# First layer of a spatial-shift mixer regrouped into three tiles of 128 channels and one of 64, with the gate logits moved to VectorE

## The chip, the cores and the metric

The kernel runs on one NeuronCore of a Trainium2 chip. The metric is device microseconds of the whole program, the median of several runs. Engine names are those of the profile: PE is TensorE, PEld its weight load, DVE is VectorE, ACT is ScalarE, POOL is GpSimd, SP is SyncE, which here does nothing but issue DMAs in order.

## What is computed

For one sequence of 2048 tokens with 448 channels, the reference mixes two branches by a gate per token:

```python
g = sigmoid((x * gate_w).sum(-1, keepdims=True))
a = A_ref(x, ...)              # S4D: long convolution over the tokens, per channel
h = gelu(layernorm(x) @ w1)    # 448 -> 448
# h in 4 groups of 112 channels, shifted by +1, -1, +2, -2 tokens
x1 = x + shifted(h) @ w2
b = x1 + gelu(layernorm(x1) @ w3) @ w4     # 448 -> 1792 -> 448
return g * a + (1 - g) * b
```

## The kernel before, in words

The tokens are taken in four blocks of 512 (`TB`). The work is a list of 72 **units**. Units 0 to 15 are the mixer, four per block, one per shift group, in the order of groups 0, 2, 1, 3. Units 16 to 71 are the MLP, 14 slices of 128 hidden channels per block. Each unit has a first layer (`first`, L437) and a second layer (`second`, L499). Precision is kept by splitting every operand into a high and a low part (`xh`+`xl`, `w1h`+`w1l`, `uh`+`ul`). A first layer is therefore 11 matmuls of 512 columns: four K tiles of `xh` with the high weights, four with the low weights, and three of `xl` with the high weights. A second layer is 12 matmuls of 448 columns: `uh` with high weights, `uh` with low weights, `ul` with high weights, for each of the four 128-token tiles `j`.

Between a unit's two layers lies a **hand-over** on two other engines. For a mixer unit DVE multiplies the PSUM result by the row of reciprocal standard deviations `rb` (`act_mul`, L446), ACT applies gelu (L456), ACT copies to the high part `uh` (L468), and DVE subtracts to get the low part `ul` (`act_tail`, L472). The main loop runs two units ahead (`LAG = 2`): its iteration n issues `first(n + 2)`, the hand-over of unit n + 2 up to `uh`, and `second(n)`. For n below 15 `act_tail(n + 1)` comes after the list `after` of iteration n, and from 15 on first of all. Every engine works its own queue strictly in the order of the program, so all that is put ahead of an `act_tail` on DVE delays the `ul` that PE waits for. At the end of a block, DVE adds the four accumulators to `xs` (L505, L508), and the next block's first `second` writes those PSUM banks again.

What comes at which iteration is written by hand, with calls `at(n, fn, ...)` in lists `before`, `after`, `between` and `late`. Four such jobs matter here. `stats_b` are LayerNorm statistics on DVE (L286, L288). `norm_turn` and `norm_fetch` transpose a tile of 128 tokens on DVE into a buffer of the two-deep pool tag `u`, write it to DRAM in two DMAs (`xd`) and read it back (`xr`). `ssm_par`, `ssm_exp`, `ssm_scale_par` and `ssm_moment` prepare the S4D branch: ACT takes an exponential of a 1 MB parameter load `pk`, DVE computes `dts` by a chain of small instructions, ACT scales by it (L580), and DVE reduces moments. `OWN = 34` is the first iteration of the S4D scans. Iterations before the fourth are written out in `begin()`.

The gate logits were an extra output column of the first layer: `w1` carried `gate_w` twice behind the 112 columns of a group, ACT copied the PSUM rows 96 to 113 of the units with group 0, and of the last with group 1 (`logits`, L540), and one row went through DRAM to `lt`. `gates()` turned it by a PE transpose, applied a sigmoid at iteration 15, and made `gs = 1 - g`. `weigh` (ACT, L410) multiplies `xs` by `gs`.

Of the kernel before, what the change touches and what calls it, by code (L numbers as in the profile page):

```python
# [24 lines left out]
GW = G + 2  # L25
# [4 lines left out]
SHIFT = (1, -1, 2, -2)  # L30
EPS = 1e-5
LAG = 2
OWN = 34
# [12 lines left out]
def gated_mix_kernel(tc, x, xT, xb, x0, w1, w2, w3, w4, par, logdt, dskip, ident, parg, uflip, lags, out):  # L46
    nc = tc.nc
    with tc.tile_pool(name="keep", bufs=1) as keep:
# [3 lines left out]
        with ExitStack() as ctx:  # L52
            mixer_and_small_steps(ctx, tc, xs, gg, okm, x, xT, xb, x0, w1, w2, w3, w4, par, logdt, dskip, ident, out)
# [121 lines left out]
def mixer_and_small_steps(ctx, tc, xs, gg, okm, x, xT, xb, x0, w1, w2, w3, w4, par, logdt, dskip, ident, out):  # L175
# [7 lines left out]
    def f32(ap):  # L183
        return ap.bitcast(F32)
# [7 lines left out]
    lg = dr.tile([1, L + 2], F32, name="lg")  # L192
# [16 lines left out]
    nu = big.tile([128, 4, 4], F32, name="nu")  # L209

# [30 lines left out]

    w1h, w1l = wpair([128, 4, 4, GW], "w1")
    w2h, w2l = wpair([G, 4, D], "w2")
    w1r = big.tile([128, 4, 4, GW], F32, name="w1r", tag="w4al")
    w2r = big.tile([128, 4, D], F32, name="w2r", tag="w4ah")

    def first_loads():
# [5 lines left out]
        act(w1r[:, 0], w1[:, 0])  # L253
        sp(r[:, :2 * HW], x0[:, :2 * HW])
        act(w1r[:, 2], w1[:, 2])
# [3 lines left out]
        sp(w1r[:, 1], w1[:, 1])  # L259
# [3 lines left out]
        sp(w1r[:, 3], w1[:, 3])  # L263
# [6 lines left out]
    def constants():  # L270
# [7 lines left out]
        nc.gpsimd.memset(carry, 0.0)  # L278
        nc.gpsimd.memset(rb[:, 0:HALO], 0.0)
# [139 lines left out]
    def first(n, bank="p1", seq=None, stop=True):  # L419
# [3 lines left out]
        if kind == "a":  # L423
            m = GW if i < 2 else G
            wh, wl = w1h[:, i, :, :m], w1l[:, i, :, :m]
            o = HALO - SHIFT[i]
        else:
            m = 128
            wh, wl = (w[:, :, i * m:(i + 1) * m] for w in (w3h, w3l))
            o = 0  # L430
# [4 lines left out]
        every = [(w, x_, k, 0, TB) for w, x_, r in ((0, 0, 4), (1, 0, 4), (0, 1, 3)) for k in range(r)]  # L435
        for q, (w, x_, k, t0, t1) in enumerate(seq or every):
            nc.tensor.matmul(p[:m, t0:t1], (wl if w else wh)[:, k, :], (xl if x_ else xh)[:, k, o + t0:o + t1],  # L437
                             start=(q == 0 and fresh), stop=stop if q + 1 == len(seq or every) else False)

    def act_mul(n):  # L440

        kind, b, i = units[n]
        m = G if kind == "a" else 128
        UF[n] = wk.tile([128, TB], F32, name="uf")
        o = b * TB + HALO - SHIFT[i]
        nc.vector.tensor_mul(UF[n][:m], P1[n][:m], rb[:m, o:o + TB])  # L446

    def act_head(n, later=False):
        kind, b, i = units[n]
        m = G if kind == "a" else 128  # L450
        UL[n] = wk.tile([128, TB], F32R, name="ul", bufs=3)
        UH[n] = wk.tile([128, TB], F32R, name="uh", bufs=3)
        if kind == "a":
            if n not in UF:
                act_mul(n)
            nc.scalar.activation(UF[n][:m], UF[n][:m], AF.Gelu_apprx_tanh)  # L456
        else:
            UF[n] = wk.tile([128, TB], F32, name="uf")
            nc.scalar.activation(UF[n][:m], P1[n][:m], AF.Gelu_apprx_tanh)  # L459
        if not later:  # L460
            act_copy(n)
        p = P1.pop(n)
        if kind == "a" and n and (i == 0 or (i == 1 and b == NB - 1)):
            logits(p, b, i)

    def act_copy(n):
        m = G if units[n][0] == "a" else 128
        nc.scalar.activation(UH[n][:m], UF[n][:m], AF.Copy)  # L468

    def act_tail(n):  # L470
        m = G if units[n][0] == "a" else 128
        nc.vector.tensor_sub(UL[n][:m], UF.pop(n)[:m], f32(UH[n][:m]))  # L472
# [9 lines left out]
    def second(n):  # L482
        kind, b, i = units[n]
        if kind == "a":
            wh, wl, m = w2h[:, i, :], w2l[:, i, :], G
            s, e = i == 0, i == 3
        else:
            wh, wl = W4[i]
            m = 128
            s, e = i == 0, i == NF - 1  # L490
        for j in range(NT):
            if s:
# [4 lines left out]
        for j, p in q:  # L497
# [550 lines left out]
```

## Time and profile before

| | us |
|---|---|
| Median of 3 runs | 380.78 (380.06 to 381.04) |
| Profiled execution | 380.4 |
| Its span in the trace | 378.6 |
| PE busy | 368.5 |
| DVE busy | 295.8 |
| ACT busy | 210.2 |

The span counts from the first to the last recorded instruction of the profiled execution; 1.8 us of its device time lie around it. Busy shares are averages over stages with different limits, so the prediction below reads single stretches. A row of the timeline gives start and duration in us, the engine and line, the operation, output and inputs with their shapes, a count, and in brackets the idle time before it with what ended it.

### The profile page before, as it was taken

The numbers are of one execution on the slowest core, as the hardware profiler recorded it, in microseconds if no ns is written. First come the engines' busy times: TensorE is split into PE (matmuls) and PEld (weight loads), VectorE is DVE, ScalarE is ACT, GpSimd is POOL, SyncE is SP. The second block draws the span as 40 slices with busy tenths as digits, with TensorE's granted clock in tenths as the row PEclk, the third lists the DMA queues.
The fourth block names the chain that finished last, engine by engine and source line by source line (L and its number), as shares of the span: only waits on it lengthen the run. The fifth ranks groups of instructions, "written<-read, shape, count | busy, mean of one in ns | idle before, by whom it ended". The sixth has DMA issues, their size and how long they took to land.

```text
span 378.6 us, 5180 instructions
## 1 busy us (share of the span) xinstructions
PE 368.5 (97%) x1713; PEld 314.6 (83%) x1713; DVE 295.8 (78%) x527; ACT 210.2 (56%) x349; POOL 71.1 (19%) x187
## 2 busy tenths in 40 slices
PE   7998999999999999999999999999999999999993
PEld 4786888888888888888888888888888888888883
DVE  4888979785858981998399989999787999996312
ACT  4764646546978467643465575465756654442220
POOL 3200070322000000040023536324041440000000
PEclk9999999999999999999999999999999999999998
DMA  8970606166615219000843515256685311372202
GB/s 266 397 265 1 224 1 173 30 118 209 209 56 157 46 50 214 3 0 12 243 72 78 83 29 153 63 160 124 97 183 134 78 28 19 73 189 48 77 0 102
DMA packets 85896, 42.26 MB, mean 112 GB/s; under 512 B 67030, under 2 KB 80614, under 8 KB 85226
## 3 DMA queue, kind: packets, MB, share of 16 engines
q1 hardware_dynamic: 85434, 41.20, 41.6%
q10 hardware_dynamic: 432, 0.70, 0.6%
q8 instruction: 15, 0.25, 0.3%
q14 instruction: 15, 0.12, 0.1%
HBM read 30.86 MB, written 11.02 MB: 111 GB/s over the span
## 4 chain that ended last, share of the span: by engine, by line
PE 90%; DVE 3%; ACT 2%; DMA 2%; issue 1%; POOL 0%; SPq 0%; DVEq 0%
PE p L437 46%; PE acc L499 43%; DMA w1r<-w_in 2%; PE acc L520 1%; ACT uh L468 1%; ACT uf L456 1%; PE misc L336 0%; DVE uf L446 0%; DVE z L638 0%; DVE w2l L218 0%; DVE b L286 0%; ACT w2h L217 0%; ACT xn L294 0%; DVE ul L472 0%; DVE xh L365 0%
## 5 line engine op out<-in xcount | busy, mean ns | idle before, releaser
L459 ACT ACTIVATE uf<-p 128x512 f32<-128x512 f32 x56 | 33.4, 597 | 101.9 <-PE p L437 101.8
L472 DVE TENSOR_TENSOR ul<-uf,uh 128x512 fp32r<-128x512 f32 (+1 forms) x72 | 48.9, 680 | 31.5 <-ACT uh L468 31.4
L638 DVE TENSOR_TENSOR_SCAN z<-z,carry 128x512 f32<-128x512 f32 x48 | 61.5, 1281 | 4.6 <-ACT z L633 0.7
L437 PE MATMUL p<-xh,w3h 128*128 128x512 f32 x224 | 61.3, 396 | 0.0
L437 PE MATMUL p<-xh,w3l 128*128 128x512 f32 x224 | 60.7, 392 | 0.0
L499 PE MATMUL acc<-w4h,uh 128*128 128x448 f32 x216 | 55.8, 364 | 0.3 <-DVE xs L508 0.3
L499 PE MATMUL acc<-w4h,ul 128*128 128x448 f32 x216 | 55.7, 364 | 0.0
L499 PE MATMUL acc<-w4l,uh 128*128 128x448 f32 x216 | 55.7, 363 | 0.0
L437 PEld LDWEIGHTS p<-xh,w3l 128*128 128x128 f32 x224 | 42.1, 188 | 9.9
L437 PE MATMUL p<-xl,w3h 128*128 128x512 f32 x168 | 48.0, 394 | 0.0
L437 PEld LDWEIGHTS p<-xh,w3h 128*128 128x128 f32 x224 | 42.0, 188 | 6.7
L468 ACT ACTIVATE uh<-uf 128x512 fp32r<-128x512 f32 (+1 forms) x72 | 45.6, 633 | 2.3
L499 PEld LDWEIGHTS acc<-w4h,uh 128*128 128x128 f32 x216 | 40.5, 188 | 6.6 <-issue 0.7
L499 PEld LDWEIGHTS acc<-w4l,uh 128*128 128x128 f32 x216 | 40.5, 188 | 3.1
L499 PEld LDWEIGHTS acc<-w4h,ul 128*128 128x128 f32 x216 | 40.5, 188 | 2.9
L633 ACT ACTIVATE z<-zs,nu 128x512 f32<-128x512 f32 x64 | 42.2, 710 | 0.8 <-DMA zs<-xT_in 0.4
L632 POOL COPY z<-carry 128x1 f32<-128x1 f32 x48 | 34.6, 731 | 17.4 <-DVE zs L644 17.1
L437 PEld LDWEIGHTS p<-xl,w3h 128*128 128x128 f32 x168 | 31.5, 188 | 7.2
L323 POOL TENSOR_TENSOR t<-r 128x4 f32<-128x4 f32 (+1 forms) x15 | 6.8, 453 | 133.2 <-DVE r L321 132.5
L640 POOL COPY carry<-z 128x1 f32<-128x1 f32 x48 | 14.1, 294 | 92.4 <-DVE z L638 91.5
L456 ACT ACTIVATE uf<-uf 112x512 f32<-112x512 f32 x16 | 10.1, 630 | 24.2 <-DVE uf L446 24.1
L638 DVE TENSOR_TENSOR_SCAN z<-z,carry,zero 128x512 f32<-128x512 f32 x16 | 20.0, 1247 | 0.0
(150 smaller groups left out, 496.5 us busy)
## 6 DMA issues: line engine op xcount, KB each, us to landing
zs<-xT_in SPq DMA_DIRECT2D x4, 1024.0 KB, 8.1
yd<-yt SPq DMA_DIRECT2D x56, 64.0 KB, 2.0
ysb<-yd SPq DMA_DIRECT2D x16, 224.0 KB, 3.0
out_dram<-xs SPq DMA_DIRECT2D x16, 224.0 KB, 2.8
raw<-xb_in SPq DMA_DIRECT2D x3, 1032.0 KB, 7.9
raw<-w_in SPq DMA_DIRECT2D x3, 1024.0 KB, 5.6
xd<-xt SPq DMA_DIRECT2D x16, 192.0 KB, 2.1
xr<-xd SPq DMA_DIRECT2D x16, 192.0 KB, 3.5
```

The costliest lines, as they stand in the source:

```text
L323: eng.tensor_mul(t, y, y)
L437: nc.tensor.matmul(p[:m, t0:t1], (wl if w else wh)[:, k, :], (xl if x_ else xh)[:, k, o + t0:o + t1], start=(q == 0 and fresh), stop=stop ...
L456: nc.scalar.activation(UF[n][:m], UF[n][:m], AF.Gelu_apprx_tanh)
L459: nc.scalar.activation(UF[n][:m], P1[n][:m], AF.Gelu_apprx_tanh)
L468: nc.scalar.activation(UH[n][:m], UF[n][:m], AF.Copy)
L472: nc.vector.tensor_sub(UL[n][:m], UF.pop(n)[:m], f32(UH[n][:m]))
L499: nc.tensor.matmul(ACC[j], (UL if p == 2 else UH)[n][:m, t], wl if p == 1 else wh, start=s and p == 0, stop=e and p == 2)
L520: nc.tensor.matmul(ACC[j], (UL if p == 2 else UH)[m][:, t], wl if p == 1 else wh, start=False, stop=m > n and p == 2)
L632: nc.gpsimd.tensor_copy(z4[:, m, 0:1], carry[:, k, m:m + 1])
L633: nc.scalar.activation(z4[:, m, 1:], ZS[b][:, k, :], AF.Copy, scale=nu[:, k, m:m + 1])
L638: nc.vector.tensor_tensor_scan(z, z, up, carry[:, k, m:m + 1], OP.add, OP.add)
L640: nc.gpsimd.tensor_copy(carry[:, k, m:m + 1], z[:, TB - 1:])
```

## The change

**Channels.** The 112 channels of group 2 (shift +2) are no longer a tile of their own. 16 of them go to the first 16 columns of each of the three other tiles, which so have 128, and the remaining 64 form the fourth tile, still the second unit of each block (units 1, 5, 9, 13). Its high and low weights stand side by side as 128 columns of one operand `w1d`, and its `uh` and `ul` stand above each other as 128 rows of one operand, against second-layer weights that are repeated in rows 64 to 127. **Fold.** The two halves of its PSUM result must be added (`act_add`): ACT copies the lower half, DVE adds.

**Edge columns.** The 16 guest channels of the other tiles need another shift than their hosts. ACT writes the gelu of the whole tile, then for rows 0 to 15 overwrites the first 1 to 4 columns from a carried tile `skew` and the other 508 to 511 columns shifted, and copies the last 4 columns to `skew`. The very first tokens get their values from four small matmuls (`first_tokens`, `first_skew`). The gelu of these units goes to a tile `ug` with one buffer.

**Gates.** `x` is read again, a tile of 448 channels for 128 tokens at a time, into the `u` buffers, and DVE sums its product with `gate_w` (`gate_sum`). The logistic function is made from Exp on ACT, and an addition and a reciprocal on DVE.

**Places.** The statistics of block 1 move from iterations 10 and 12 to 15 and 16; the second half of the S4D preparation moves two iterations later, and so does `OWN`; `begin()` is reordered.

```diff
-        every = [(w, x_, k, 0, TB) for w, x_, r in ((0, 0, 4), (1, 0, 4), (0, 1, 3)) for k in range(r)]
+        every = [(w, x_, k, 0, TB) for w, x_, r in ((0, 0, 4), (1, 0, 4), (0, 1, 3)) for k in range(r)
+                 if not w or wl is not None]
...
+    def act_add(n):
+        p = P1[n]
+        UF[n] = wk.tile([128, TB], F32, name="uf")
+        nc.scalar.activation(UF[n][:GD], p[GD:], AF.Copy)
+        nc.vector.tensor_add(UF[n][:GD], p[:GD], UF[n][:GD])
...
     def act_head(n, later=False):
...
-            nc.scalar.activation(UF[n][:m], UF[n][:m], AF.Gelu_apprx_tanh)
+            o, sk = SHIFT[2] - SHIFT[i], skew[:, TI[i], :]
+            uf, UF[n] = UF[n], big.tile([128, TB], F32, name="ug", tag="w4bl")
+            nc.scalar.activation(UF[n], uf, AF.Gelu_apprx_tanh)
+            nc.scalar.activation(UF[n][:GX, :o], sk[:, SKEW - o:], AF.Gelu_apprx_tanh)
+            nc.scalar.activation(UF[n][:GX, o:], uf[:GX, :TB - o], AF.Gelu_apprx_tanh)
+            if b + 1 < NB:
+                nc.scalar.activation(sk, uf[:GX, TB - SKEW:], AF.Copy)
...
-        if kind == "a" and n and (i == 0 or (i == 1 and b == NB - 1)):
-            logits(p, b, i)
...
     def act_tail(n):
...
+        if kind == "a" and i == 2:
+            nc.vector.tensor_sub(UH[n][GD:], uf[:GD], f32(UH[n])[:GD])
...
-        q = [(j, p) for p in range(3) for j in range(NT)]
+        q = [(j, p) for p in range(2 if kind == "a" and i == 2 else 3) for j in range(NT)]
...
+    def gate_fetch(j):
+        GX_[j] = wk.tile([128, 512], F32, name="gx", tag="u")
+        nc.sync.dma_start(GX_[j][:, :D], x[j * 128:(j + 1) * 128])
+
+    def gate_sum(j):
+        t = GX_.pop(j)[:, :D]
+        nc.vector.scalar_tensor_tensor(t, t, 1.0, GR[0], op0=OP.mult, op1=OP.mult, accum_out=gg[:, j:j + 1])
...
     def gates():
-        p = ps.tile([128, L // 128], F32, name="misc", bufs=1)
-        nc.tensor.transpose(p, LT[0], idt[:L // 128, :L // 128])
-        nc.scalar.activation(gg, p, AF.Sigmoid)
+        nc.scalar.activation(gg, gg, AF.Exp, scale=-1.0)
+        nc.vector.tensor_scalar(gg, gg, 1.0, None, op0=OP.add)
+        nc.vector.reciprocal(gg, gg)
...
+        first(3, "misc", wh_wl[5:])
+        first_tokens()
...
+        keep_warm(2)
...
+        act_add(5)
         stats_b(2 * NT + 1, 2 * NT + 3)
         act_head(4)
...
-    for b, (n, m, q) in enumerate(((5, 6, 6), (10, 12, 12), (27, 28, 29), (34, 35, 36))):
+    for b, (n, m, q) in enumerate(((5, 6, 6), (15, 16, 17), (27, 28, 29), (34, 35, 36))):
...
+    for j, n in zip(range(L // 128), (16, 16, 17, 17, 19, 19, 20, 20, 23, 23, 24, 24, 25, 25, 26, 26)):
+        at(n, gate_fetch, j, when=late)
+        at(n + 1, gate_sum, j)
...
-    at(25, ssm_exp, 1)
+    at(27, ssm_exp, 1)
+    at(27, gates)
...
+                if units[n + LAG][::2] == ("a", 2):
+                    act_add(n + LAG)
```

How the instructions stand at three places follows, from the order of the program on each engine; a row is the line, the operation, the output and inputs, and the output's shape.

**First place: PE, the first layer of unit 5**, the second unit of block 1 (`p_423` before, `p_442` of the change). Before:

```order
L437 MATMUL p_423<-xh,w1h 112x512 x4
L437 MATMUL p_423<-xh,w1l 112x512 x4
L437 MATMUL p_423<-xl,w1h 112x512 x3
```

Of the change:

```order
L450 MATMUL p_442<-xh,w1d 128x512 x4
L450 MATMUL p_442<-xl,w1d 128x512 x3
```

The four matmuls with the low weights are gone, since those are columns of `w1d`.

**Second place: DVE at the end of `begin()`**, from the last row of the second rstd to the accumulators of block 0. Before:

```order
L310 SCALAR_TENSOR_TENSOR r_82<-t,r_82 128x4
L286 BN_STATS b_441<-xs 128x6 x2
L288 BN_AGGR st<-b_441 128x2 x2
L446 TENSOR_TENSOR uf<-p_392,rb 112x512
L446 TENSOR_TENSOR uf<-p_423,rb 112x512
L472 TENSOR_TENSOR ul<-uf,uh 112x512
L505 TENSOR_TENSOR xs<-acc_316,xs 128x448
```

Of the change:

```order
L324 SCALAR_TENSOR_TENSOR r_81<-t,r_81 128x4
L512 TENSOR_TENSOR ul<-ug,uh 128x512
L457 TENSOR_TENSOR uf<-p_442,uf 64x512
L300 BN_STATS b_459<-xs 128x6 x2
L302 BN_AGGR st<-b_459 128x2 x2
L473 TENSOR_TENSOR uf<-p_408,rb 128x512
L469 TENSOR_TENSOR uf<-uf,rb 64x512
L512 TENSOR_TENSOR ul<-ug,uh 128x512
L544 TENSOR_TENSOR xs<-acc_330,xs 128x448
```

The tail of unit 3 (`ul` in the second row) and the fold of unit 5 (`p_442`) now stand ahead of the multiplication of unit 4 (`p_408`).

**Third place: the DMA queue of SP at iterations 19 and 20.** `xd` are the transposed tiles on their way to DRAM, `xr` is their way back, `gx` the second read of `x`. Before:

```order
L390 DMA xd<-xt 128x3x128
L392 DMA xd<-xt 128x64
L390 DMA xd<-xt 128x3x128
L392 DMA xd<-xt 128x64
L397 DMA xr<-xd 128x12x32
L400 DMA xr<-xd 64x4x32 x2
```

Of the change:

```order
L404 DMA xd<-xt 128x3x128
L406 DMA xd<-xt 128x64
L404 DMA xd<-xt 128x3x128
L406 DMA xd<-xt 128x64
L584 DMA gx<-x_in 128x448 x2
L411 DMA xr<-xd 128x12x32
L414 DMA xr<-xd 64x4x32 x2
```

Two reads of `x` come between the two ways, into the buffers that the `xt` tiles leave.

More of the change, by code (lines that the diff above doesn't have):

```diff
@@ L480, in done, with second @@
             nc.sync.dma_start(out[q * 128:(q + 1) * 128], xs[:, q, :])
-    def second(n):
+    def second(n, part=slice(0, None)):
         kind, b, i = units[n]
         if kind == "a":
-            wh, wl, m = w2h[:, i, :], w2l[:, i, :], G
+            wh, wl = w2h[:, i, :], w2l[:, i, :]
             s, e = i == 0, i == 3
@@ L719, in keep_warm @@
         for _ in range(m):
-            nc.tensor.matmul(p[:GW], w1h[:, 0, 0, :], XH["a", 0][:, 0, :TB], start=True, stop=True)
+            nc.tensor.matmul(p, w1h[:, 0, 0, :], XH["a", 0][:, 0, :TB], start=True, stop=True)
     PS = []
```

242 lines of the change are left out of this document (142 added, 100 removed).

## The prediction

> **What bounds the kernel now.** I read the page's busy times and slices first, then its chain of work that ended last, then the groups of waits, then the timelines of PE and DVE between 35 and 152 us, where the change acts.
>
> ```profile
> PE 368.5 (97%) x1713; PEld 314.6 (83%) x1713; DVE 295.8 (78%) x527; ACT 210.2 (56%) x349; POOL 71.1 (19%) x187
> PE   7998999999999999999999999999999999999993
> PEclk9999999999999999999999999999999999999998
> PE 90%; DVE 3%; ACT 2%; DMA 2%; issue 1%; POOL 0%; SPq 0%; DVEq 0%
> ```
>
> PE is busy for 97% of the span, at full clock, and holds 90% of the chain. So a matmul taken away is worth its whole length, provided that what the others hand to PE is early enough to keep it fed. How early that is, three stretches of one mixer block each show (columns: stretch, its us, then busy us of PE, PEld, DVE, ACT, POOL):
>
> ```profile
> 38.13:58.43 20.30, 20.30 (x98) 17.14 (x96) 16.96 (x38) 11.86 (x21) 7.08 (x26) 1.00 0.33 112
> 58.43:78.61 20.18, 20.18 (x96) 17.03 (x95) 16.60 (x34) 10.81 (x18) 3.90 (x12) 1.00 0.38 100
> 78.61:98.80 20.19, 20.19 (x94) 17.08 (x93) 14.15 (x26) 13.19 (x19) 4.70 (x14) 1.00 0.63 171
> ```
>
> PE never stops there, but DVE works 14 to 17 of 20 us, and its remaining time is mostly waiting for ACT, since a unit passes DVE, ACT, ACT, DVE in turn. This second chain is close behind PE.
>
> **The change part by part: matmuls removed (A).**
>
> ```profile
> 43.23 2.55 PE p L437 x11
> 50.79 2.42 PE acc L499 x12
> ```
>
> A first layer takes 2.55 us for 11 matmuls, 0.232 each; a second layer 2.42 us for 12, 0.202 each. The four units with 64 channels lose four matmuls in each layer: 16 x 0.232 + 16 x 0.202 = 3.7 + 3.2 = **6.9 us**. Every other unit keeps its counts, as the duration of a matmul follows its columns and not its rows. The four small matmuls of the first tokens, two fewer of `keep_warm` and the lost PE transpose of the gates I take together at 0; between nothing and 0.3 us each way, as they stand where PE waits for data in the start.
>
> **The hand-over of units 4 to 15 (B).**
>
> ```profile
> L446 DVE TENSOR_TENSOR uf<-p,rb 112x512 f32<-112x512 f32 x16 | 10.9, 686 | 3.4 <-ACT rb L337 3.1
> L456 ACT ACTIVATE uf<-uf 112x512 f32<-112x512 f32 x16 | 10.1, 630 | 24.2 <-DVE uf L446 24.1
> L472 DVE TENSOR_TENSOR ul<-uf,uh 112x512 fp32r<-112x512 f32 x16 | 11.0, 685 | 3.4 <-ACT uh L468 3.3
> L540 ACT ACTIVATE lr<-p 18x512 f32<-18x512 f32 x5 | 3.0, 592 | 0.1
> L555 ACT ACTIVATE gg<-misc 128x16 f32<-128x16 f32 x1 | 0.2, 185 | 0.0
> L288 DVE BATCH_NORM_AGGREGATE st<-b 128x2 f32<-128x6 f32 x28 | 4.2, 174 | 0.1
> ```
>
> The row of 18x512 shows that a copy of 18 rows costs ACT 592 ns, near the 630 ns of a gelu of 112 rows: ACT is paid by columns. The shifted gelu of 16 rows by 508 to 511 columns is thus estimated at 0.66 us, like a full one, and the one of 1 to 4 columns at 0.10 to 0.19 us (the 128x16 row is 185 ns). Together **0.76 us** more between gelu and copy, in all units but the 64-channel ones; bounds 0.69 and 0.85.
>
> By the Trainium skill ("ScalarE: Activation LUTs", section "Rules for kernel authors") an ACTIVATE costs about 0.3 us and 0.83 ns per element. That would make the pair an estimated 1.02 us, and add about 1.6 us over the six waits; the 592 and 185 ns of the two rows speak for less.
>
> Next I followed the DVE order of the change from unit 4 to unit 15 with such durations, and compared each moment with before. The rows that carry it:
>
> ```profile
> 36.55 1.29 DVE L446 TENSOR_TENSOR uf<-p,rb 112x512 f32<-112x512 f32 x2
> 38.61 0.69 DVE L472 TENSOR_TENSOR ul<-uf,uh 112x512 fp32r<-112x512 f32 x1 [0.76 <-ACT uh L468]
> 54.32 0.69 DVE L446 TENSOR_TENSOR uf<-p,rb 112x512 f32<-112x512 f32 x1 [1.41 <-ACT rb L337]
> 80.38 1.15 DVE L286 BATCH_NORM_STATS2 b<-xs 128x6 f32<-128x448 f32 x2
> 95.62 1.29 DVE L472 TENSOR_TENSOR ul<-uf,uh 112x512 fp32r<-112x512 f32 x2
> 96.79 0.36 PE L499 MATMUL acc<-w2h,ul 112*128 112x448 f32 x1
> ```
>
> Terms, as later (+) or earlier (-) along DVE. At the start +0.2: the tail of unit 3 and the fold come ahead of the multiplication of unit 4 (+2.5), but the second rstd stands 2.3 us earlier. The row at 38.61 shows DVE waiting 0.76 us for ACT already, so ACT's added work comes straight out at the tails: 0.73, 0.5, 0.55, 0.14, 0.45, 0.14 and 0.9 us at units 4, 6, 7, 8, 10, 12 and 14 to 15, in all +3.4. The folds of units 9 and 13 are one DVE operation of 0.7 each, +1.4. Two subtractions of weights and `xl`, whose high parts ACT now copies later, +1.1. Against this, the wait of 1.41 us for `rb` at unit 8 is taken up (-1.4), and two calls of block 1's statistics leave (each 1.15 + 2 x 0.17 = 1.5, by the row at 80.38), -2.9. Sum 0.2 + 3.4 + 1.4 + 1.1 - 4.3 = **+1.8 us at the tail of unit 15**. In before this tail ends at 96.9 - 0.6 = 96.3, as the two that begin at 95.62 take 1.29 with their overlap, and PE takes that `ul` at 96.79: 0.5 us to spare. So unit 15's second layer ends **1.3 us later** than before, though PE has 6.9 us less to do: the hand-over eats all of A, in stalls that I put at 2.4 us ahead of the second layer of unit 4 and 1 to 1.5 us ahead of 8, 11, 12 and 15. Bounds: the saving comes through whole (-6.9), or 0.85 for the edges and nothing credited for `rb` (+3.5).
>
> **The S4D preparation (C).**
>
> ```profile
> 109.37 0.16 DVE L573 TENSOR_SCALAR dts<-dts 128x4 f32<-128x4 f32 x1
> 109.55 1.71 ACT L580 ACTIVATE pk<-pk,dts 128x256 f32<-128x256 f32 x4 [2.44 <-DVE dts L573]
> 111.28 1.28 ACT L459 ACT_TABLE_LOAD   x1
> 112.57 0.60 ACT L459 ACTIVATE uf<-p 128x512 f32<-128x512 f32 x1
> 113.21 0.63 ACT L468 ACTIVATE uh<-uf 128x512 fp32r<-128x512 f32 x1
> 113.87 0.69 DVE L472 TENSOR_TENSOR ul<-uf,uh 128x512 fp32r<-128x512 f32 x1 [4.34 <-ACT uh L468]
> 116.25 0.97 PE L499 MATMUL acc<-w4h,uh 128*128 128x448 f32 x4
> L668 DVE SCALAR_TENSOR_TENSOR xs<-ysb,gg,xs 128x448 f32<-128x448 f32 x16 | 10.1, 672 | 0.0
> L594 DVE DVE_READ_ACCUMULATOR mw<-mw 128x1 f32 x12 | 1.0, 82 | 0.0
> ```
>
> ACT stands still for `dts`, then scales, loads a table and only then forms `uf` and `uh` of unit 19: `uh` is there 113.84 - 109.53 = 4.3 us after `dts`, and PE takes it at 116.25, 2.4 us later. Ahead of `dts` on DVE now come the moved statistics (2.9 us with their rstd's share 0.4: 3.3) and two sums of gates, each like the 672 ns row and an 82 ns read, 1.5 with gaps; 1.1 of it fits into idle time, and DVE is 1.8 behind from B: 3.3 + 1.5 - 1.1 + 1.8 = 5.5, of which I take 5.2 as the statistics partly overlap. PE is 1.3 late and has 2.4 of slack: 5.2 - 1.3 - 2.4 = **+1.5 us**. Bounds 0 (DVE waits elsewhere give it back) and 2.5.
>
> **The gates (D).**
>
> ```profile
> xd<-xt SPq DMA_DIRECT2D x16, 192.0 KB, 2.1
> ysb<-yd SPq DMA_DIRECT2D x16, 224.0 KB, 3.0
> 120.01 0.39 SPq L390 DMA_DIRECT2D xd<-xt  x1
> 121.72 0.68 DVE L472 TENSOR_TENSOR ul<-uf,uh 128x512 fp32r<-128x512 f32 x1
> 139.33 0.65 DVE L472 TENSOR_TENSOR ul<-uf,uh 128x512 fp32r<-128x512 f32 x1
> 140.93 0.39 SPq L565 DMA_DIRECT2D pk<-par_in  x1
> 142.54 0.69 DVE L472 TENSOR_TENSOR ul<-uf,uh 128x512 fp32r<-128x512 f32 x1 [1.36 <-ACT uh L468]
> 146.37 0.63 ACT L568 ACTIVATE pk<-pk 128x512 f32<-128x512 f32 x1 [2.56 <-DMA pk<-par_in]
> 147.98 0.69 DVE L586 TENSOR_REDUCE rho<-pk 128x2 f32<-128x512 f32 x1 [4.74 <-ACT pk L580]
> ```
>
> The fetches of tiles 4 and 5 wait for the `u` buffers until the `xd` transfers have read them (120.01 + 2.1, in before's time), and land 3.0 us after (the row of the same 224 KB), near 125.1. DVE comes to their sums right behind the tail of unit 21, at 122.4 to 122.8: a new wait of some 2.3 us, with the tails of 22 and 23 and eight moment operations behind it, on which ACT in turn depends. SP's queue holds the `xr` issues behind these two fetches, so they move by up to 1.6 us as well. The fetches of tiles 8 and 9 stand behind the 1 MB `pk`, which took 146.37 - 140.93 = 5.4 us, while DVE reaches their sums near 140 to 141, after the tail at 139.33: a wait of 4 to 6 us. Part falls into idle time that is there (1.36 and 4.74 us in these rows), and the tails of 22 to 28 have some 5 to 9 us to spare, so that not all reaches PE. Last, the Exp of the gates on ACT waits for the sixteenth sum, with the gelu of unit 29 behind it, about 2 us. Traced to the end the delays give 0 to +6; I take **+3.5**, a little over the middle, because two of the three waits follow each other inside ten units and the slack can be spent only once. Sixteen sums (12 us of DVE) are otherwise hidden, and so is the S4D queue moved by two units: DVE idles at the end.
>
> **Sum:** 380.4 (profiled execution, 0.4 under the median) + 1.3 + 1.5 + 3.5 = 386.7; with up to 0.3 us back from the start, **386.5 us**.
>
> **The rivals.** *PE stays the bound*: DVE's idle time before the tails hides the edge work, PE runs through, and the gates fit into idle time. 380.4 - 6.9 + 0.5 = **374.0**, faster. It decides if the tail of unit 15 lands before PE reaches the third matmul of that unit, that is if B's +1.8 is in truth about -5. For it: DVE's busy time per block leaves 3 to 6 us. Against: most of those are waits for ACT, which gets longer. If half of A comes through and the rest is hidden, it is 377.
>
> *Only the mixer's hand-over counts*: A eaten, C and D lie in DVE's idle time (4.34, 1.36 and 4.74 us in the rows above), 380.4 + 1.3 = **381.7**, between 378.5 and 383.
>
> *The clock falls*. In before the slices show full clock and the longest wait of PE in the mixer is 1.1 us; here stalls of 2.4 us, up to 3.9, would stand. If the clock halved for one first layer after such a stall, 2.55 us would be added to the forecast: 386.5 + 2.5 = **389.0**.
>
> ```profile
> 35.23 0.65 PE L336 MATMUL misc<-idt,r 128*128 128x128 f32 x4 [1.15 <-DVE r L310]
> ```
>
> The Trainium skill ("TensorE: Matmul & The Clock Gate", section "What's actually happening") says that an idle window of about 3.4 us halves the clock. No stall of before is long enough to show it.
>
> **How the numbers follow.** My forecast, a hand-over that eats A plus stalls in units 17 to 29 (383 to 390.5), has 0.56; PE-bound 0.20 (half of it under 377); only the mixer 0.16; the clock 0.05; beyond 390.5, 0.03. The range of **377 to 390.5** leaves out 0.10 below and 0.03 above. A measurement tells 0.3%, or 1.1 us, from no change: 379.6 to 381.9 holds 0.09, about half of the second rival; faster is the first rival and a part of the second, 0.24; slower is the rest, 0.67.
>
> **What would show it.** A: PE's busy time falls by 7. B: PE idle ahead of the second layers of 4, 8, 11, 12 and 15, released by `ul` or the accumulators' addition; if unit 15 ends near 92 us, the first rival holds. C: ACT idle longer than 2.44 us for `dts`, and PE waiting ahead of unit 19. D: DVE idle with `gx` as releaser at tiles 4, 5, 8 and 9; if there is none, the second rival. A clock under 1.00 in any slice after 40 us shows the third. The forecast is wrong above all if the edge operations cost much less than a full gelu.

## The result, and the profile after

The changed kernel takes 396.07 us (395.88 to 397.36), the kernel before 380.91 in the same session: ratio 1.041, interval 1.038 to 1.044. It is **slower by 15.2 us**. Slower was forecast, but at 386.5 us and in a range that ended at 390.5.

The rows of the page that answer to the first ones of before:

```profile
PE 368.3 (93%) x1686; PEld 311.6 (79%) x1686; DVE 309.2 (78%) x568; ACT 215.2 (55%) x379; POOL 73.5 (19%) x193
PE   7989799889999998698999999999999999999994
PEclk9999899999999999899999999999999999999999
PE 62%; DVE 18%; ACT 9%; DMA 6%; issue 3%; SPq 0%; DVEq 0%; ACTq 0%
```

PE issues 27 instructions fewer, but is busy as long as before, since time at half its clock counts as busy too (without any such time it was busy 364.5 us in the first run below); it has holes in slices 5, 8, 9, 16, 17 and 19 (9.85 us each), and its clock fell in the fifth and the seventeenth. It holds 62% of the chain instead of 90%; DVE, ACT and DMA took the rest. Who stopped whom, from the groups of waits (total, times, longest):

```profile
ACT xn L396 <- DVE xh L388: 8.1, 4, 6.9
DVE gx L588 <- DMA gx<-x_in: 13.0, 5, 7.1
ACT pk L618 <- DVE dts L611: 5.9, 1, 5.9
PE p L450 <- DVE w3l L224: 3.9, 1, 3.9
PE acc L538 <- DVE xs L544: 2.4, 1, 2.4
PE acc L538 <- DVE ul L512: 2.4, 3, 1.2
```

PE waits for DVE, and DVE waits 13.0 us for tiles of `x` that it did not need before. The main stalls behind the start, in order of time, from PE's timeline (idle time ahead of the row and what ended it in brackets):

```profile
41.64 0.71 PE L538 MATMUL acc<-w2h,uh 128*128 128x448 f32 x1 [2.41 <-DVE xs L544]
77.24 0.47 PE L538 MATMUL acc<-w2h,ul 128*128 128x448 f32 x1 [1.24 <-DVE ul L512]
83.38 0.44 PE L538 MATMUL acc<-w2h,uh 128*128 128x448 f32 x1 [1.33 <-ACT uf L481]
100.18 0.47 PE L538 MATMUL acc<-w2h,ul 128*128 128x448 f32 x1 [0.81 <-DVE ul L512]
120.28 1.08 PE L538 MATMUL acc<-w4h,uh 128*128 128x448 f32 x4 [0.41 <-ACT uh L504]
146.87 1.08 PE L538 MATMUL acc<-w4h,uh 128*128 128x448 f32 x4 [0.92 <-ACT w4h L223]
149.27 1.09 PE L538 MATMUL acc<-w4l,uh 128*128 128x448 f32 x4 [1.32 <-DVE w4l L224]
160.97 2.04 PE L450 MATMUL p<-xh,w3l 128*128 128x512 f32 x4 [3.92 <-DVE w3l L224]
185.94 0.44 PE L538 MATMUL acc<-w4h,uh 128*128 128x448 f32 x1 [1.56 <-DVE xs L547]
```

The first four rows lie ahead of or inside the second layers of units 4, 11, 12 and 15 in the mixer, the fifth is unit 19, the others are in the stretch with the gates. Where the loss had come to by then is read from one landmark in both traces, the first matmuls of the second layer of unit 17 (end of the mixer) and of unit 31 (end of the gates). In before:

```profile
106.33 0.97 PE L499 MATMUL acc<-w4h,uh 128*128 128x448 f32 x4
175.78 0.97 PE L499 MATMUL acc<-w4h,uh 128*128 128x448 f32 x4
```

In the changed kernel:

```profile
109.80 0.98 PE L538 MATMUL acc<-w4h,uh 128*128 128x448 f32 x4
190.99 0.97 PE L538 MATMUL acc<-w4h,uh 128*128 128x448 f32 x4
```

So 3.5 us are lost by unit 17 and 15.2 by unit 31; from there to the end 0.3 more. Of the 11.7 us between the two landmarks, 8.5 are stalls of PE. The clock is read from the windows view (the number ahead of the last two is the granted clock):

```profile
42.00:44.00 2.00, 2.00 (x6) 1.76 (x6) 2.00 (x5) 1.51 (x3) 0.00 (x0) 0.50 0.00 0
162.00:164.00 2.00, 2.00 (x6) 1.61 (x5) 0.18 (x2) 0.63 (x1) 0.00 (x0) 0.50 0.85 241
```

Right behind the stalls of 2.41 and of 3.92 us, PE runs at half its clock: 6 matmuls in 2 us instead of 10 or 11. The trace records each such stretch as 3.41 us long, so it takes 1.7 us from PE. How much of that is left at the end is another matter. The first stretch can be priced against the first run below, which has the same stall without it: unit 5 starts 1.65 us later here (48.22 against 46.57), but unit 17 only 0.5 (109.80 against 109.28), because in between PE waits for the hand-over anyway.

How D came about is seen in DVE's rows:

```profile
131.14 0.62 DVE L588 SCALAR_TENSOR_TENSOR gx<-gx,gr 128x448 f32<-128x448 f32 x1 [2.59 <-DMA gx<-x_in]
158.95 0.63 DVE L588 SCALAR_TENSOR_TENSOR gx<-gx,gr 128x448 f32<-128x448 f32 x1 [7.08 <-DMA gx<-x_in]
160.23 1.29 DVE L224 TENSOR_TENSOR w3l<-raw,w3h 128x512 fp32r<-128x512 f32 x2
```

The sum of tile 4 waits 2.59 us, that of tile 8 waits 7.08, and right behind the second stands a split of first-layer weights that PE needs at once: the 3.92 us at 160.97.

### The profile page after: what moved, and what is told of

The parts are those of the page before. It is cut to its first block, busy times and chain, and to the rows that moved or that the text cites. A ratio compares the mean times of both kernels' runs of the same rounds, so it can differ in the third digit from the quotient of the medians.

```text
span 394.1 us, 5240 instructions
## 1 busy us (share of the span) xinstructions
PE 368.3 (93%) x1686; PEld 311.6 (79%) x1686; DVE 309.2 (78%) x568; ACT 215.2 (55%) x379; POOL 73.5 (19%) x193
## 4 chain that ended last, share of the span: by engine, by line
PE 62%; DVE 18%; ACT 9%; DMA 6%; issue 3%; SPq 0%; DVEq 0%; ACTq 0%
PE acc L538 30%; PE p L450 30%; DMA gx<-x_in 4%; DVE ul L512 2%; DVE w4l L224 2%; DVE gx L588 2%; ACT uh L504 1%; DMA raw<-x_in 1%; PE acc L559 1%; DVE b L300 1%; DVE w3l L224 1%; ACT ug L486 1%; DVE uf L473 1%; DVE mw L630 1%; ACT ug L488 1%
## 5 line engine op out<-in xcount | busy, mean ns | idle before, releaser
L450 PE MATMUL p<-xh,w3l 128*128 128x512 f32 x224 | 62.0, 398 | 3.9 <-DVE w3l L224 3.9
L538 PE MATMUL acc<-w4h,uh 128*128 128x448 f32 x216 | 56.8, 368 | 3.1 <-DVE xs L547 1.8
L512 DVE TENSOR_TENSOR ul<-uf,uh 128x512 fp32r<-128x512 f32 x56 | 38.1, 680 | 23.2 <-ACT uh L504 23.1
L504 ACT ACTIVATE uh<-uf 128x512 fp32r<-128x512 f32 x56 | 35.5, 633 | 1.8
L337 POOL TENSOR_TENSOR t<-r 128x4 f32<-128x4 f32 (+1 forms) x15 | 5.1, 338 | 141.9 <-DVE r L335 141.2
L538 PE MATMUL acc<-w2h,uh 128*128 128x448 f32 x64 | 20.1, 382 | 5.5 <-DVE xs L544 2.4
L486 ACT ACTIVATE ug<-uf 128x512 f32<-128x512 f32 x12 | 7.6, 632 | 22.9 <-DVE uf L473 22.9
```

The costliest lines, as they stand in the source:

```text
L450: nc.tensor.matmul(p[:, t0:t1], (wl if w else wh)[:, k, :], (xl if x_ else xh)[:, k, o + t0:o + t1], start=(q == 0 and fresh), stop=stop i ...
L486: nc.scalar.activation(UF[n], uf, AF.Gelu_apprx_tanh)
L504: nc.scalar.activation(UH[n], UF[n], AF.Copy)
L512: nc.vector.tensor_sub(UL[n], uf, f32(UH[n]))
L538: nc.tensor.matmul(ACC[j], (UL if p == 2 else UH)[n][:, t], wl if p == 1 else wh, start=s and p == 0, stop=e and p == 2)
```

## The experiments

All are edits of the changed kernel, and the diffs show their main lines. A landmark table, starts of second layers in us, with the stretches of halved clock up to unit 31 by their lengths in the trace:

```
                      unit 4   unit 13  unit 17  unit 31  halved clock
before                 40.66    86.11   106.33   175.78   none
changed kernel         41.64    88.42   109.80   190.99   3.41, 3.41
no sums, no edges      39.83    82.17   102.03   171.56   none
no sums                41.51    87.94   109.28   178.82   none
fetches, no sums       41.72    88.33   109.69   180.64   3.41
sums of resident data  41.62    88.42   109.77   185.24   3.41, 3.41
sums, no edges         39.58    81.91   101.76   183.05   3.41
last mended order      38.93    84.53   107.22   177.43   none
```

### What the gates cost

**No sums at all.**

```diff
+        nc.gpsimd.memset(gg, 0.0)
...
-        at(n, gate_fetch, j, when=late)
-        at(n + 1, gate_sum, j)
+        pass
```

> The changed kernel with the sixteen fetches and sums of the gates left out (the gate column is zero, so the gates are all one half). Theory Q (the loss behind unit 17 comes from DVE standing still for the fetched tiles, with weight splits and block additions queued behind): units 17 to 30 lose at most 2 us instead of 11.7, no clock drop near 160 us, about 385 us. Rival W (it is the 12 us of DVE work, not the waits): also about 385 here; the next run tells the two apart. Rival S (it is the S4D work moved by two units): still above 392.

384.32 us, ratio 1.009 (1.007 to 1.012). From unit 17 to unit 31 nothing is lost any more (2.95 and 3.04 us behind the kernel before). The gates are worth 396.07 - 384.32 = 11.75 us, and the moved S4D work nothing up to there.

**Other fetch dates.**

```diff
-    for j, n in zip(range(L // 128), (16, 16, 17, 17, 19, 19, 20, 20, 23, 23, 24, 24, 25, 25, 26, 26)):
+    for j, n in zip(range(L // 128), (16, 16, 17, 17, 20, 20, 21, 21, 22, 22, 24, 24, 25, 25, 26, 26)):
```

> The changed kernel with the fetches of tiles 4 to 9 at iterations 20 to 22 instead of 19 to 23, so that none stands right behind a transposed tile or the 1 MB parameter load; all sixteen sums stay. Theory Q: the waits of 2.6, 0.8 and 7.1 us of DVE for fetched tiles go, and with them PE's 2.2 us at unit 24, 3.9 us for weights and 1.7 us of halved clock: 386 to 389 us. Rival W: DVE is as full as before, 393 to 396.

397.30 us (1.042 to 1.048): no gain, against theory Q's number and above W's too. The trace does not show W either, for the waits had only moved. DVE's longest is now:

```profile
162.84 0.63 DVE L588 SCALAR_TENSOR_TENSOR gx<-gx,gr 128x448 f32<-128x448 f32 x1 [9.20 <-DMA gx<-x_in]
```

In SP's queue that fetch stands behind the `xr` issues, which went on until 159.5 us. So this run could not tell work from waits; the next two could.

**Sums without fetches.**

```diff
-        t = GX_.pop(j)[:, :D]
-        nc.vector.scalar_tensor_tensor(t, t, 1.0, GR[0], op0=OP.mult, op1=OP.mult, accum_out=gg[:, j:j + 1])
+        t = wk.tile([128, 512], F32, name="gx", tag="u")
+        nc.vector.scalar_tensor_tensor(t[:, :D], xs[:, j, :], 1.0, GR[0], op0=OP.mult, op1=OP.mult,
+                                       accum_out=gg[:, j:j + 1])
...
-        at(n, gate_fetch, j, when=late)
```

> The changed kernel with its sixteen sums at their iterations, but taken from the resident tiles of x (in which the mixer's additions already stand, so the gates are those of other values); no tile is fetched again, so DVE has the same work and no transfer to wait for. Theory Q (the waits): 385 to 387 us, units 17 to 30 lose at most 2.5. Rival W (9 to 11 us more work on a full DVE): 391 to 396, with PE's stalls ahead of units 24 and 30 still there.

389.08 us (1.018 to 1.025): 4.8 us above the run without sums, so Q and W each have a part. (One wait of DVE stayed, 1.17 us for a `u` buffer that an `xd` transfer still read.) Where W's part lies is plain in PE's timeline of this run:

```profile
178.62 0.44 PE L538 MATMUL acc<-w4h,uh 128*128 128x448 f32 x1 [2.61 <-DVE xs L547]
```

Unit 30 waits 2.61 us for the additions of block 0 on DVE, and half the clock follows for 3.41 us. From unit 17 to unit 28 only 0.9 us had been lost.

**Fetches without sums.**

```diff
+        nc.gpsimd.memset(gg, 0.0)
...
-        at(n + 1, gate_sum, j)
```

> The changed kernel with the sixteen fetches and no sum (the gate column is zero). What is left is the transfers, their place in SP's queue and the buffers that they hold. Theory Q with W: near 385, since DVE waits for nothing. Rival X (the fetches delay the transposed tiles behind them in SP's queue, and through them ACT and PE): 387 to 392, with PE waiting where ACT copies the fetched-back tiles.

385.93 us (1.012 to 1.017), 1.6 above no fetches. So by the medians, of the 11.75 us of the gates **1.6** are the transfers by themselves, **4.8** DVE's own work, and the remaining **5.4** appear only with both: DVE standing still for a fetched tile, and what stands behind it. The landmarks of unit 17 and unit 31 leave out what differs ahead of the gates and behind them; by them the parts are 1.4, 5.9 and 4.3 (the stretch takes 69.5 us without either, 70.9 with the fetches, 75.5 with the sums and 81.2 with both). The last two each hold one stretch of halved clock. The split is thus good to about 1 us.

**Sums early, from resident tiles.**

```diff
+        gate_sum(0)
+        gate_sum(1)
         act_add(5)
...
+        gate_sum(2)
+        gate_sum(3)
         act_tail(4)
...
-        at(n, gate_fetch, j, when=late)
-        at(n + 1, gate_sum, j)
+    for j in range(NT, L // 128):
+        at(min(j, 14), gate_sum, j)
```

> The first of these edits alone: sums from the resident tiles, four in the start and twelve in iterations 4 to 14, each right ahead of a subtraction that waits for ACT. If they fit into those waits: the mixer ends within 1.5 us of 102.5, and units 17 to 30 lose nothing as they do without sums, 384 to 387 us. If not, each of the sixteen adds up to 0.55 us on the hand-over: the mixer ends at 106 to 110 and the whole at 389 to 394.

386.02 us (1.012 to 1.017): behind unit 17 nothing is lost (5.2 us behind the kernel before there, 5.3 at unit 31), as expected. The mixer ends at 104.2, 1.7 us behind 102.5 and so just outside what was expected if the sums were free. The whole computation costs 10 us less than in the changed kernel, with no read of `x` and with sums at other places.

### What the edges cost

**No edges.**

```diff
-            nc.scalar.activation(UF[n][:GX, :o], sk[:, SKEW - o:], AF.Gelu_apprx_tanh)
-            nc.scalar.activation(UF[n][:GX, o:], uf[:GX, :TB - o], AF.Gelu_apprx_tanh)
-            if b + 1 < NB:
-                nc.scalar.activation(sk, uf[:GX, TB - SKEW:], AF.Copy)
```

> The changed kernel without the two shifted gelu operations and the copy of the last columns of the twelve tiles of 128 channels (so the sixteen guest channels keep their hosts' shift). Theory E (the hand-over through ACT eats the saved matmuls): PE's stalls ahead of units 11, 12 and 15 go, the one ahead of unit 4 falls under 1.9 us and its clock drop goes; the mixer ends near 96 to 97.5 us instead of 102.5, the whole near 390 to 391. Rival F (the fold and the subtractions on DVE set it, ACT has room): the mixer ends within 1 us of 102.5.

388.96 us (1.021 to 1.026), 7.1 less. By the landmark the mixer ends 8.0 us earlier (101.76 against 109.80) and 4.6 ahead of the kernel before, further than E expected. From there to unit 31 the gates take 11.8 us, as in the changed kernel (11.7).

**Neither.**

The edits are those of "no sums" and of "no edges" together.

> The changed kernel without the sums and fetches of the gates (half for every gate) and without the shifted gelus (guests keep their hosts' shift): the regrouped matmuls with neither of the two things that pay for them. If the two losses are separate, 384.3 minus the 7.1 of the edges alone is 377; with nothing else in the way, the first rival's 374. Above 380 a third cost would be left that neither theory has.

375.85 us, ratio 0.987 (0.986 to 0.989), **faster than before** by 4.8 (1.3%). PE is busy 97% of the span again:

```profile
PE 362.9 (97%) x1686; PEld 309.7 (83%) x1686; DVE 299.8 (80%) x536; ACT 206.2 (55%) x346; POOL 74.7 (20%) x194
```

So the removed matmuls are real, and the fold with its 128-row hand-over lets most of them through. Two things spoil it: the edges, 384.32 - 375.85 = 8.5 us, and the gates, 11.75.

The edge operations cost what was estimated, as ACT's rows of the changed kernel show:

```profile
38.86 0.20 ACT L487 ACTIVATE ug<-skew 16x1 f32<-16x1 f32 x1
38.97 0.61 ACT L488 ACTIVATE ug<-uf 16x511 f32<-16x511 f32 x1
39.48 0.19 ACT L490 ACTIVATE skew<-uf 16x4 f32<-16x4 f32 x1
39.61 0.63 ACT L504 ACTIVATE uh<-ug 128x512 fp32r<-128x512 f32 x1
```

From 38.86 to the copy at 39.61 are 0.75 us. Between 102.03 and 109.28 at unit 17 lie 7.3 us; 0.9 of them are there at unit 3 already (32.98 and 33.92), from the edges of the first units. The other 6.3 are 0.70 for each of the nine units with edges behind it (4, 6, 7, 8, 10, 11, 12, 14, 15): nearly every one is paid in full.

### Order or length

**One swap.**

```diff
+        second(3)
         act_tail(4)
-        second(3)
```

> The changed kernel with the DVE subtraction of unit 4 placed behind the additions of block 0 instead of ahead of them, nothing else. If the stall ahead of unit 4 and the clock drop behind it come from the additions standing behind a subtraction that waits for ACT: the wait of 2.4 us falls to 1 or less, the clock stays at 1.00 there, and unit 4 ends 3 us earlier. If all of that reaches the end, 393 us; if the next waits for ACT are absolute in time, only 1 to 2 us are left at unit 15, 394 to 395.

395.17 us (1.036 to 1.042). The stall fell to 1.06 and 0.50 us and the clock stayed up in the mixer, but unit 13 is only 1.2 us and unit 31 1.0 us earlier: the next waits took it.

**Statistics back.**

```diff
-    for b, (n, m, q) in enumerate(((5, 6, 6), (15, 16, 17), (27, 28, 29), (34, 35, 36))):
+    for b, (n, m, q) in enumerate(((5, 6, 6), (10, 12, 12), (27, 28, 29), (34, 35, 36))):
```

> The changed kernel with the statistics of block 1 back at iterations 10 and 12. By the step that credited 2.9 us for their leaving: the mixer ends 1.5 to 3 us later than 102.5, and ACT's wait for dts is 3 us shorter at its end; with unit 19 no longer late, 395.5 to 398. If DVE waits for ACT there anyway: the mixer ends as before and the whole is 394.5 to 396.

397.41 us (1.042 to 1.051). Unit 17 starts 2.1 us later than in the changed kernel (111.86 in its trace): their leaving is worth about 2, not the 2.9 credited. That difference is not of the statistics alone: here unit 4's stall has no halved clock behind it, but one of 1.80 us at unit 12 has. ACT's wait for `dts` shrinks from 5.9 to 5.2 only.

**Four fixes with early sums.**

```diff
+        second(3)
         act_tail(4)
-        second(3)
...
+    for j in range(NT, L // 128):
+        at(min(j, 14), gate_sum, j)
...
-        at(m, sp3, c, 0, when=between if c == 0 else after)
+        at(m, sp3, c, 0, when=between if c < 2 else after)
...
+            if b == 0 and i < 2:
+                when = between
```

> The changed kernel with four edits: the sums taken from the resident tiles of x before the mixer adds to them (in iterations 4 to 14 and before), block 0's additions ahead of unit 4's subtraction, the first two transposed tiles' copies and subtractions behind unit 11's subtraction instead of ahead, and one weight split behind unit 15's instead of ahead. If order, and not amount, of DVE's work is what costs: the mixer ends at 96 to 100 us instead of 102.5, nothing is lost behind it, 376 to 381. If DVE is simply too full there: the mixer ends above 102 and the whole is above 384.

385.15 us (1.010 to 1.017): no better end of the mixer (109.93), with a stall of 2.34 us at unit 12 and a halved clock behind it. By the numbers expected this speaks for a DVE that is too full there; the next run leaves the sums out.

**Mended order, no sums.**

```diff
+                if n in (7, 11):
+                    second(n)
                 if units[n + LAG][::2] == ("a", 2):
                     act_add(n + LAG)
...
-            n = s0 + (3, 4, 5, 3)[b] * (i // 2)
+            n = s0 + (4, 4, 5, 3)[b] * (i // 2)
```

> The changed kernel without the fetches and sums of the gates (half for every gate), and with the order on DVE and ACT mended in five places: the additions of blocks 0, 1 and 2 ahead of the subtraction or the fold that they stood behind, two statistics of the start one iteration later, the second pair of transposed tiles one iteration later, the copies and subtractions of all four behind the next unit's subtraction, and one weight split behind unit 15's. Without the mending it is 384.3. If the saved matmuls are lost to what stands in front of DVE's and ACT's hand-overs: the mixer ends at 94 to 98 us instead of 102, 376 to 380. If the three operations more per hand-over are too long in themselves: it still ends above 100 and the whole is above 382.

385.08 us (1.010 to 1.014), a miss with a cause of its own. Unit 13 starts 1.3 us ahead of before (84.78); then the transposed tiles, which this edit had moved, are late:

```profile
91.57 2.25 PE L451 MATMUL p<-xh,w3h 128*128 128x512 f32 x4 [5.00 <-ACT xh L421]
```

**Second pair of tiles earlier**, without and with sums.

```diff
-                at(n, norm_d, b, i, when=between)
+                at((7, 8)[i // 2], norm_d, b, i, when=between)
+                at((8, 9)[i // 2], norm_turn, b, i, when=(after, late)[i // 2])
```

> As the run with the mended order (fetches and sums of the gates left out, half for every gate), but the second pair of transposed tiles is turned two iterations earlier instead of one later, so that the MLP's first layer does not wait for it. There the mixer was 2.1 us ahead of the kernel before at unit 13 and lost 7 us to that one wait. If order is what eats the saved matmuls: 1.5 to 3 us ahead at unit 15 and 377 to 379.5 in all, faster than before. If the hand-over with its three operations more is too long however it is ordered: at or behind the kernel before at unit 15, 381 or more.

> The same order with all sixteen sums, so that the whole computation is there: fourteen from the resident tiles of x, where DVE waited for ACT in the run before, and two fetched at iteration 16. If sums in such waits are free: within 1.5 us of the run without them, 378 to 381. If each still costs its 0.55 us: 384 to 388, slower than the kernel before.

389.79 (1.022 to 1.026) and 389.83 us (1.022 to 1.027): two misses. Now the first pair is late, and behind it on DVE the additions of block 2: in the first of the two runs PE stands 3.71 us for them, and then 2.52 us for the second pair.

**Tiles where they were**, ACT's copies in a better place, without and with sums.

```diff
+    for i in (2, 3):
+        at(11, norm_d, 0, i, when=before)
...
+            if b == 0:
+                q, when = (10, 13)[i // 2], between
```

> The mended order once more, without fetches and sums (half for every gate), with the transposed tiles at the iterations that they had: ACT forms the second pair of normalized tiles right behind the row of reciprocal deviations and ahead of unit 12's gelu. If order is what eats the saved matmuls: the mixer at least 1 us ahead of the kernel before at unit 15, no stall above 1.5 us, 378 to 380.5. If at or behind it, 381 or more, the hand-over's length is too much in this order too.

> The same with all sixteen sums (fourteen from the resident tiles, in iterations 5 to 7, 10, 13 and 14 and in the start; two fetched at iteration 16), the whole computation. Free sums: within 1.5 us of the run without them. Sums at their full 0.55 us: 6 to 9 us above it.

385.50 (1.012 to 1.015) and 384.46 us (1.009 to 1.012). Without sums unit 13 starts at 84.43, 1.7 ahead, then PE stands 4.07 us for the second pair, so that this run does not decide between order and length either. The run with sums showed something new in POOL's rows, the same operation beside a DVE without and with sums:

```profile
70.55 0.20 POOL L340 TENSOR_SCALAR t<-t 128x3 f32<-128x3 f32 x1
70.83 0.49 POOL L341 TENSOR_TENSOR r<-r,t 128x3 f32<-128x3 f32 x1
71.40 0.59 POOL L338 TENSOR_TENSOR t<-r 128x3 f32<-128x3 f32 x1
72.06 0.59 POOL L339 TENSOR_TENSOR t<-t,v 128x3 f32<-128x3 f32 x1
72.74 0.58 POOL L340 TENSOR_SCALAR t<-t 128x3 f32<-128x3 f32 x1
73.41 0.53 POOL L341 TENSOR_TENSOR r<-r,t 128x3 f32<-128x3 f32 x1
```

From 70.65 on DVE makes four sums in a row, and POOL's 0.20 us become 0.5 to 0.6; in the run without sums the rows from 70.71 to 71.82 all take 0.19 to 0.20.

**Copies one iteration earlier**, without and with sums (the diff is against the two runs before).

```diff
-                q, when = (10, 13)[i // 2], between
+                q, when = (10, 12)[i // 2], between
```

> The last mended order without fetches and sums (half for every gate), with one more change: ACT copies the second pair of transposed tiles, and DVE subtracts, one iteration earlier, ahead of unit 14's gelu, where both waited before. In the run before, the mixer was 2.5 us ahead of the kernel before at unit 13, then PE stood 4.07 and 0.89 us for these copies and lost 3.4 us to the halved clock. If order is what eats the saving: 2 to 4 us ahead at unit 15, no clock below 1.00 in the mixer, 376 to 378.5. If length: behind at unit 15, 381 or more.

> The same with all sixteen sums, the whole computation; no sum runs while POOL forms the last reciprocal deviations, because POOL's small operations took 0.49 to 0.59 us instead of 0.19 to 0.20 beside them. Twelve from the resident tiles, four fetched at iterations 16 and 17. Free sums: 377 to 380, faster than the kernel before. Each at 0.55 us: 384 or more.

383.45 (1.006 to 1.010) and 385.48 us (1.010 to 1.015). The clock stays at 1.00 in both. Without sums unit 17 is 1.8 behind before: two weight splits stand ahead of the tails of units 14 and 15. With sums it is 2.0 us more. In the four pairs of runs with and without sums that are placed early (up to four of the sixteen still fetched), the sums cost 1.7 us (in the order of the changed kernel), 0.0, -1.0 and 2.0, with different stretches of halved clock in them; where the change put them it is 11.75.

**Splits behind the tails.** (This edit comes on top of those of the run before without sums.)

```diff
-            at(m + (f // 2 if i < 2 else 0), sp4, i, f)
+            at(m + (f // 2 if i < 2 else 0), sp4, i, f, when=after if i else between)
```

> As the run before without sums (half for every gate), with the two splits of second-layer weights in iterations 13 and 14 placed behind the subtractions of units 14 and 15 on DVE instead of ahead of them. There the mixer was 2.2 us ahead at unit 13, and PE then stood 0.68, 0.68 and 1.29 us while DVE waited 2.95 and 3.02 us for ACT's copies of those weights. If order is what eats the saving: 1 to 2.5 us ahead of the kernel before at unit 15 and 378.5 to 381. If another wait takes the place of these at once: still behind at unit 15, 382 or more.

382.79 us (1.004 to 1.009), between the two cases expected. Unit 15's second layer ends 0.9 us ahead of before, against 3.0 behind without any mending. Then the next wait:

```profile
102.20 0.44 PE L539 MATMUL acc<-w4h,uh 128*128 128x448 f32 x1 [1.61 <-DVE xs L545]
107.22 0.98 PE L539 MATMUL acc<-w4h,uh 128*128 128x448 f32 x4
```

Unit 16 waits for the additions of block 3, which now stand behind the moved statistics on DVE, and unit 17 starts at 107.22, 0.9 behind before. So the order that was tried was worth 109.28 - 107.22 = 2.1 us by then (3.9 at unit 15). With the edges left out unit 17 starts at 102.03; how much of the 5.2 us between is the length of the hand-over, and how much an order that was not found, no run shows. No complete kernel of these beats the kernel before; the nearest is 384.46 us. Whether yet another order would beat it was not tried.

## Why the prediction was wrong

- **A, 6.9 us of matmuls: about right.** Without edges and sums 4.8 come through to the end, and PE is busy 5.6 us less. In the changed kernel itself the sign that was named, PE's busy time down by 7, does not show, in part because of the halved clock (364.5 against 368.5 in the run without sums).
- **B, the hand-over: right in kind, too small.** Forecast +1.3 at unit 15. Measured +3.0 in the run without sums, where the clock stays up, and +3.5 in the changed kernel. The stalls were named ahead of 4, 8, 11, 12 and 15; they came at 4, 11, 12 and 15 in the profile after, and at 8 too in the run without sums. The failed term is "in all +3.4" for the edges, half of what nine units at 0.76 make, as if DVE's other work covered the rest: the runs give 7.3 by unit 15, 0.9 of it from the start. Their price per unit was right (0.75 against 0.76), but a hand-over that the next one waits for carries it on, nine times. The 1.02 us that the prediction sets beside it from a quoted budget were too high, as it expected: 0.61 and 0.20 us were measured. The other terms together were too high: without edges they give 1.8 - 3.4 - 0.5 = -2.1, and in the run with neither edges nor sums unit 15's second layer ends 4.3 earlier than before (94.70 against 98.96). So two errors partly cancel, 1.3 + 3.9 - 2.2 = 3.0, and the forecast of B came nearer than its parts deserve. Which of the other terms (start, folds, subtractions, the wait for `rb`, the statistics) was too high no run separates.
- **C, the S4D preparation: too large.** Forecast +1.5; ACT waits 5.90 us for `dts` instead of 2.44, but PE was itself 3.5 late and stood only 0.41 us; the loss at unit 19 is 0.7 (nothing without sums).
- **D, the gates: the step that failed.** Forecast +3.5 with bounds 0 to 6, measured 15.2 - 3.5 - 0.7 = 11.0. The waits were there where they were put: 2.59 us at tile 4 and 0.80 at tile 5 (2.3 forecast), 7.08 at tile 8 (4 to 6 forecast), and ACT stood 2.7 us for the sixteenth sum (about 2 forecast). What failed is the step that "the tails of 22 to 28 have some 5 to 9 us to spare, so that not all reaches PE": it counted the slack of the tails alone. Behind the sums stand also the splits `w4l` and `w3l` and the subtractions of the transposed tiles, for which ACT waits 6.93 us with the next unit's gelu behind it; these had no such slack, and PE stopped for `w4l` 1.32 us and for `w3l` 3.92. And "Sixteen sums (12 us of DVE) are otherwise hidden" failed too: by themselves they cost 4.8, since they push the additions of block 0 into PE's way, though they take 8.8 us of DVE and not 12 (309.2 us busy against 300.4).
- **The clock**, a rival at 0.05, happened, and twice. It had been priced at 2.5. The first time cost 0.5 by unit 17, the second at most 1.7: at most 2.2 of the 15.2 us.
- **The first rival** is what the run with neither edges nor sums does: 375.85 against its 374.0. Its condition (the edge work hidden) does not hold in the changed kernel. The second rival, only the mixer's hand-over, is ruled out by the 11.7 us that are lost between units 17 and 31.

The Trainium skill ("TensorE: Matmul & The Clock Gate", section "What's actually happening") has a free-running window of 3413 ns, and this case agrees: every stretch of halved clock in the table is 3.41 us or, in others of these runs, 6.83, and the stretches of full clock between them last 34 and 67 times 3.413 us in the changed kernel. Where the prediction quotes the same section for an idle window of about 3.4 us, the measurements differ: 1.80 to 2.41 us of idle time in one window were enough here (last section).

What stays open: how the 4.3 to 5.4 us that sums and fetches cost only together divide among the weight splits, ACT's wait and the second clock drop, and whether any order with edges can beat the kernel before.

## What to carry to other kernels

Work that is moved onto an engine that is not the bound must be checked against everything queued behind it there, weight splits and copies for other engines too, and not against the slack of the one hand-over in view; a wait for a DMA in such a queue is paid by all of them. A fixed addition to a serial hand-over is to be counted once per hand-over, not once per stretch, as soon as the chain has no slack. Where PE never waited before, a stall forecast at about 2 us can halve its clock behind it; how much of that lasts depends on whether PE or the hand-over sets the pace behind it (1.65 us at unit 5 here, 0.5 at unit 17).

## What the hardware showed that was not expected

- A PE stall of 2.40 to 2.42 us ahead of unit 4 was followed by 3.41 us of halved clock in the changed kernel and in three of its variants (sums of resident data, fetches without sums, early sums), and by none in three others (no sums, other dates, statistics back). The clock changed only on a grid of 3.413 us, and what tells the two cases apart is how much idle time of PE lies in one step of it. In the windows view, the step around the stall and the next one, in the changed kernel and then without sums:

```profile
38.15:41.57 3.42, 1.08 (x5) 0.56 (x3) 1.84 (x4) 3.31 (x8) 0.00 (x0) 1.00 0.00 0
41.57:44.98 3.41, 3.34 (x9) 3.02 (x10) 3.40 (x6) 1.95 (x4) 0.00 (x0) 0.50 0.00 0
36.42:39.83 3.41, 2.68 (x12) 1.88 (x10) 2.14 (x6) 1.74 (x5) 0.00 (x0) 1.00 0.00 0
39.83:43.25 3.42, 1.74 (x9) 1.65 (x10) 3.11 (x6) 3.39 (x7) 0.00 (x0) 1.00 0.00 0
```

  In the first, 2.34 us of the stall fall into one step and the next is halved. In the second, a line of the grid cuts the stall into 0.73 and 1.68, and the clock stays. Worked out in this way (idle is where the profile has no matmul running) for all kept traces, from the first full clock on, every step at full clock with 1.95 us or more of idle time was followed by a halved one and none with 1.75 or less; between them one of 1.80 was (statistics back, unit 12) and those of 1.81 and 1.83 were not. Where the grid lies against the kernel differs between these runs, so the same stall cost clock in one and none in another.
- POOL's operations on 128x3 elements took 0.49 to 0.59 us instead of 0.20 while DVE ran operations with two inputs in SBUF, and PE waited 3.27 us for their chain instead of 1.48. The Trainium skill ("GPSIMD Engine Reference", section "1. Specifications") names such contention with VectorE instructions that have two SBUF inputs; the rows agree.
